# Load order, piece shapes and zero matmuls at the start of a cross-attention and maxout kernel

## The chip, the cores and the metric

The kernel runs on one core of one Trainium2 chip. The metric is the device time of one execution in microseconds (us); before the change it is 150.77 us (median of 3 runs, 150.74 to 151.8). TensorE is called PE here, its weight loads PEld, VectorE DVE, ScalarE ACT, GpSimd POOL; SyncE (SP) issues nearly all DMAs.

## What is computed

The reference, cut to what matters (B=8, H=8, S=512, Ns=32, D=64; the second part has d_model 512 and d_ff 1024):

```python
def _attn_ref(x, state):                       # x: B,H,S,D   state: B,H,Ns,D
    scores = scale * np.matmul(x, state.transpose(0, 1, 3, 2))
    ...                                        # softmax over the 32 state rows: a
    xread = np.matmul(a, state)
    scores2 = scale * np.matmul(state, x.transpose(0, 1, 3, 2))
    ...                                        # softmax over the 512 rows of x: a2
    sread = np.matmul(a2, x)
    return np.concatenate([xread, sread], axis=2)

def _moe_ref(x, w1, w2, w_out):                # x: 8 * 544 rows of 512
    h1 = x @ w1
    h2 = x @ w2
    g = np.maximum(h1, h2)
    return (g @ w_out)
```

The kernel uses max(h1, h2) = max(h1 - h2, 0) + h2. So it needs the difference of the two weights, `wd` = W1 - W2, and the product `wwo` = W2 Wo, and the output is relu(x wd) Wo + x wwo.

## The kernel before, in words

All loads are float32 and all matmuls take bfloat16. x is loaded per batch in two halves of four heads (`load_x(b, g)`, 512 KB each, runs of 1 KB in a partition). The weights come in pieces: `PIECES` (L19) gives for each of four pieces of W1 and of W2 the columns of d_ff and the blocks of 128 rows of d_model, 512 KB each, and Wo comes in quarters `load_wo(q)` of two blocks of 128 rows of d_ff. State is loaded for batch 0, for batch 1 and for batches 2 to 7.

The steps, by the short names that the order table uses:

- `ce` casts two heads of x to bfloat16 (`cast_e`, L209); `xt` transposes four heads on PE (8 matmuls), `xte` copies them out of PSUM. `cS`, `S`, `Se` do the same for the state.
- `sc` scores (8 matmuls), `exp` their exponential on ACT, `red` the sums and reciprocals on DVE, `mul` the normalised weights a; `at`/`ate` transpose a and copy it out. `sr`, `sre`, `srt`, `srte` are the read of x by the state. These give attention's parts of one batch.
- `cw2` casts a piece of W2, `w2` transposes it on PE (8 matmuls), `w2e` copies it to `w2m`. `cwo` casts a quarter of Wo. `ww.i.q` is two matmuls of the product `wwo`, for the block i of d_model and quarter q of d_ff; `wwe` copies a finished block.
- `sub.k.h` is half of piece k of the difference `wd` (`w_sub`, L414).
- `sw.b.z` multiplies the state of batch b by a range z of columns of `wd` (or, z = w, by `wwo`), 8 matmuls; `swe` copies it to `sw_s`. `CHUNKS` (L21) says which ranges batches 0 and 1 have.
- `l1.b.f` is two matmuls (L332) for block f of d_ff, `re` their relu. `l2.b.c.q` is two matmuls (L346) over quarter q, and `l2.b.c.o` two (L341) with `wwo`; five of them make an output block, which `le` copies out and `store` stores.

The work of batches 0 and 1 and of the preparation is not in a loop. The table `ORDER` (L23 to L46) is the order in which the instructions are issued; each engine gets its part of it in this order and waits in order. `@` gives the PSUM bank, `>` the engine (V, A, P for DVE, ACT, POOL). The loop for batches 2 to 7 follows (L573 on), and in it one l1 of 8 blocks, one l2 of 4 and the attention of the next batch. `idle` (L423) multiplies zeros, and `idle.9@0` at the start of the order is 9 such matmuls of 512 columns. `RELEASE` is the order in which the loop takes the eight banks.

The order of DMAs is that of SP's queue. Slots of `big` are used in turn: the fifth batch's x goes into the slot in which the first half of W2's columns was.

Of the kernel before, what the change touches and what calls it, by code (L numbers as in the profile page):

```python
# [23 lines left out]
cw2.2>P ldw2.1 sc.0.1@0 red.0.0>V exp.0.1>A w2.2@1 mul.0.0>P cw2.3>A sr.0@0 red.0.1>V ldw2.0 mul.0.1>P sre.0>V w2.3@2
cwo.3>A ldwo.0 w2e.2>V srt.0@0 at.0.0@3 srte.0>A sub.3.0>V w2e.3>A ldwo.1 sub.3.1>V ldw1.0 ate.0.0>A ww.2.3@2
sub.2.0>V ldw1.1 at.0.1@1 cS.1.2>A ww.3.3@3 ww.1.3@0 sub.2.1>V ate.0.1>A ldS.2.8 S.1.2@4 sw.0.1@1,5 Se.1.2.1>V
ce.1.3>A Se.1.2.0>V ce.1.2>P sw.1.1@4,6 swe.0.1.1>V ww.0.3@7 swe.0.1.0>A swe.1.1.0>V xt.1.1@5 swe.1.1.1>A ce.1.1>P
l1.0.7@1 ce.1.0>A xte.1.1>V l1.0.4@6 l1.0.6@4 re.0.7>A re.0.4>V cwo.2>P xt.1.0@5 re.0.6>A sc.1.1@1 l1.0.5@6 xte.1.0>V  # L30
exp.1.1>A ww.3.2@3 re.0.5>A sc.1.0@1 red.1.1>V ww.1.2@0 exp.1.0>A ww.2.2@2 cw2.1>V ww.0.2@7 l2.0.1.2@1 mul.1.1>P
ldx.3.1 red.1.0>V w2.1@6 cw2.0>A l2.0.2.2@5 mul.1.0>P w2e.1>V l2.0.2.3@5 l2.0.1.3@1 cwo.0>V w2.0@6 at.1.1@4 ww.2.0@2
w2e.0>V ldx.2.1 ww.3.0@3 cwo.1>P ate.1.1>V ww.0.0@7 ww.1.0@0 sub.0.1>V ldx.2.0 ww.3.1@3 at.1.0@4 ldx.3.0 sub.0.0>V
ww.0.1@7 wwe.3>A ww.1.1@0 sub.1.1>P ate.1.0>V wwe.0>A ww.2.1@2 wwe.1>V l1.1.7@7 wwe.2>A sr.1@4 sub.1.0>V re.1.7>A
sw.0.w@2,0 sre.1>V sw.0.0@3,6 swe.0.w.1>A l1.1.5@7 swe.0.w.0>V l1.1.6@4 swe.0.0.1>A mS.1>P l1.1.4@0 re.1.5>A re.1.6>V
l2.0.0.2@6 re.1.4>A l2.0.1.o@1 swe.0.0.0>V ce.3.2>P sw.1.0@4,7 mS.0>A sw.1.w@3,0 ce.3.3>P swe.1.0.1>V l2.0.0.3@6
swe.1.w.1>A cb.3.1>P Sd l1.0.0@2 swe.1.0.0>V l1.0.1@7 swe.1.w.0>A re.0.0>V l2.0.3.2@4 cb.2.1>P re.0.1>A l2.0.2.o@5
l1.1.1@2 ce.3.0>P l2.0.1.0@1 re.1.1>V l1.0.2@7 cb.2.0>P l1.1.3@3 re.0.2>V l2.0.3.o@4 re.1.3>A ce.3.1>P xtd.2 l1.1.0@2
ce.2.1>P l2.0.3.0@4 re.1.0>A srt.1@3 l2.0.0.0@6 ldx.4.0 cb.3.0>P srte.1>V l1.0.3@2 l2.0.0.o@6 re.0.3>A ce.2.2>P
l2.0.3.3@4 xtd.3 l1.1.2@2 ce.2.0>P l2.0.1.1@1 re.1.2>A ce.2.3>P l2.1.3.2@3 le.0.1>V l2.1.3.3@3 l2.1.3.1@3 l2.1.3.0@3  # L40
l2.1.2.2@1 ldx.4.1 l2.1.0.o@2 sc.2.1@7 l2.0.3.1@4 exp.2.1>A sc.2.0@0 l2.0.0.1@6 exp.2.0>A red.2.1>V l2.1.0.0@2
le.0.3>A l2.1.0.3@2 red.2.0>V mul.2.1>P l2.1.0.2@2 l2.1.2.3@1 le.0.0>V l2.1.2.o@1 mul.2.0>P l2.1.0.1@2 l2.0.2.0@5
le.1.0>A atd.2 l2.1.2.1@1 l2.0.2.1@5 l2.1.3.o@3 le.0.2>A l2.1.2.0@1 le.1.3>V sw.2.1@5,2 store.0 le.1.2>A sw.2.0@6,4
swe.2.1.0>V sw.2.w@3,0 swe.2.1.1>A sr.2@1 swe.2.0.0>V l2.1.1.3@5 swe.2.w.1>A l2.1.1.o@5 sre.2>V swe.2.0.1>A l2.1.1.2@5
l2.1.1.1@5 swe.2.w.0>V srt.2@1 l2.1.1.0@5 srte.2>V le.1.1>A
# [628 lines left out]
```

## Time and profile before

| what | us |
|---|---|
| median of 3 runs | 150.77 |
| the profiled execution's own time | 150.94 |
| its span, first to last instruction | 149.0 |
| around the span | 1.94 |
| PE busy in the span | 138.1 |
| from the start to the first l1 of batch 2 | 54.82 |
| from there to the end | 94.2 |

The tables of windows in the prediction give for a stretch of the span: its length, then for PE, PEld, DVE, ACT and POOL the busy time and the count of instructions, the clock granted to TensorE (1.00 is full), the busy share of the DMA engines, and GB/s. Rows of the timeline give the start, the duration, the engine, the line, the operation and, in brackets, how long the engine had been idle and what ended that; "x2" merges instructions that follow each other. In a row that starts after a wait for a DMA, the start is the landing of that DMA, within some 0.05 us. The chain's rows give start, duration and the step that the end was waiting for.

### The profile page before, as it was taken

To read this page: it belongs to the slowest core of one execution; us is meant where nothing else is said; L and a number is where in the kernel's file an instruction comes from. 1 tells how busy PE (TensorE), PEld (TensorE's weight loads), DVE (VectorE), ACT (ScalarE), POOL (GpSimd) and SP (SyncE) were. 2 spreads that over 40 slices of the span, in tenths; PEclk is the share of its full clock that TensorE was granted. 3 is DMA by queue.
4 is the path that set the end of the run, shared out by engine and by line. 5 is a ranking of instruction groups with operands and counts; after the bars stand their busy time and mean duration, and the time that the engine had idled before them with its cause. 6 is when DMAs were issued, how large, how long until landed. Compare 5 with 4: busy or idle time off the path is not lost.

```text
span 149.0 us, 3067 instructions
## 1 busy us (share of the span) xinstructions
PE 138.1 (93%) x1205; PEld 68.9 (46%) x1224; DVE 83.3 (56%) x163; ACT 66.1 (44%) x120; POOL 53.0 (36%) x81
## 2 busy tenths in 40 slices
PE   6846979999999999999999999999999999999990
PEld 2435446434445445444544454454445344754460
DVE  3567876796415367583855485376637586640120
ACT  3258673387324557045632745181547135511100
POOL 4352147497913700735091437056500500000000
PEclk9987999999999999999999999999999999999999
DMA  4999999996996568986969598779306033302332
GB/s 137 255 396 362 370 387 378 283 342 93 189 246 200 106 248 297 129 208 230 235 145 290 234 114 189 264 282 145 70 31 255 7 66 141 145 0 96 115 140 80
DMA packets 36063, 29.44 MB, mean 198 GB/s; under 512 B 23120, under 2 KB 31568, under 8 KB 35152
## 3 DMA queue, kind: packets, MB, share of 16 engines
q1 hardware_dynamic: 35776, 29.17, 69.9%
q8 instruction: 10, 0.16, 0.4%
q10 hardware_dynamic: 272, 0.07, 0.2%
q14 instruction: 5, 0.04, 0.1%
HBM read 15.20 MB, written 8.91 MB: 162 GB/s over the span
## 4 chain that ended last, share of the span: by engine, by line
PE 81%; DMA 10%; SPq 3%; DVE 1%; issue 1%; POOL 1%; ACT 0%
PE bank L346 38%; PE bank L332 17%; PE bank L341 9%; DMA big<-in_moe_w_out_dram 7%; PE bank L309 4%; PE bank L460 3%; DMA big<-in_x_dram 3%; SPq L155 3%; PE bank L365 2%; PE bank L375 2%; PE bank L240 2%; PE bank L280 1%; PE bank L373 1%; DVE wd L417 1%; POOL wo L103 1%
## 5 line engine op out<-in xcount | busy, mean ns | idle before, releaser
L346 PE MATMUL bank<-wo,r 128*128 128x512 bf16 (+1 forms) x259 | 61.4, 372 | 0.5
L346 PEld LDWEIGHTS <-r 128*128 128x128 bf16 x264 | 25.4, 98 | 28.5 <-issue 0.3
L99 ACT COPY big<-bank 128x512 f32<-128x512 f32 (+1 forms) x17 | 9.7, 573 | 47.1 <-PE bank L346 47.1
L332 PE MATMUL bank<-at,sw 128*128 128x512 bf16 x126 | 30.0, 379 | 0.1
L256 POOL TENSOR_TENSOR a<-e,er 128x512 bf16<-128x512 bf16 x16 | 16.7, 1065 | 36.3 <-ACT e L248 16.0
L327 DVE TENSOR_SCALAR r<-bank 128x512 bf16<-128x512 f32 x29 | 20.0, 691 | 15.9 <-PE bank L332 15.5
L325 ACT ACTIVATE r<-bank 128x512 bf16<-128x512 f32 x35 | 21.2, 608 | 8.2 <-PE bank L332 8.0
L101 DVE CAST sw<-bank 128x512 bf16<-128x512 f32 x24 | 15.3, 685 | 9.4 <-PE bank L309 9.3
L103 POOL CAST xe<-big 128x512 bf16<-128x512 f32 x28 | 16.4, 620 | 10.0 <-DMA big<-in_x_dram 10.0
L332 PEld LDWEIGHTS <-sw 128*128 128x128 bf16 x128 | 12.0, 98 | 14.0 <-issue 0.2
L101 DVE COPY big<-bank 128x512 f32<-128x512 f32 (+1 forms) x16 | 10.5, 654 | 13.6 <-PE bank L346 11.2
L341 PE MATMUL bank<-sw,at 128*128 128x512 bf16 (+1 forms) x56 | 17.1, 372 | 0.3
L103 POOL CAST xb<-big 128x1024 bf16<-128x1024 f32 x12 | 12.3, 1041 | 12.1 <-issue 11.4
L252 DVE TENSOR_REDUCE sums<-e 128x16 f32<-128x512 bf16 x16 | 10.6, 664 | 4.5 <-ACT e L248 4.4
L99 ACT CAST sw<-bank 128x512 bf16<-128x512 f32 x24 | 12.7, 599 | 0.2
L248 ACT ACTIVATE e<-bank 128x512 bf16<-128x512 f32 x16 | 9.0, 595 | 4.9 <-PE bank L240 4.5
L460 PE MATMUL bank<-wo,w2m 128*128 128x512 bf16 x30 | 7.8, 379 | 1.9 <-ACT w2m L99 1.2
L341 PEld LDWEIGHTS <-at 128*128 128x128 bf16 x66 | 5.7, 97 | 5.3
L240 PEld LDWEIGHTS <-xt 128*128 128x128 bf16 x128 | 5.1, 98 | 2.6 <-DVE xt L101 0.7
L240 PE MATMUL bank<-sbd,xt 128*128 128x64 bf16 x128 | 5.5, 193 | 0.6 <-DVE xt L101 0.6
L309 PE MATMUL bank<-wd,sbd 64*32 64x512 bf16 x128 | 5.8, 382 | 0.3 <-DVE sbd L101 0.2
L101 DVE COPY w2m<-bank 128x1024 bf16<-128x1024 bf16 (+1 forms) x4 | 2.8, 689 | 5.1 <-PE bank L375 4.1
(71 smaller groups left out, 105.1 us busy)
## 6 DMA issues: line engine op xcount, KB each, us to landing
big<-in_x_dram SPq DMA_DIRECT2D x14, 512.0 KB, 5.1
out_dram<-big SPq DMA_DIRECT2D x7, 1024.0 KB, 6.0
big<-in_moe_w_dram SPq DMA_DIRECT2D x8, 512.0 KB, 10.2
big<-in_moe_w_out_dram SPq DMA_DIRECT2D x4, 512.0 KB, 10.3
big<-in_x_dram SPq DMA_DIRECT2D x1, 1024.0 KB, 5.4
out_dram<-big SPq DMA_DIRECT2D x1, 512.0 KB, 2.6
out_dram<-w2m SPq DMA_DIRECT2D x2, 256.0 KB, 2.4
sf<-in_state_dram SPq DMA_DIRECT2D x1, 384.0 KB, 11.0
```

The lines of the kernel that those rows point to most:

```text
L99: nc.scalar.copy(o, i)
L101: nc.vector.tensor_copy(o, i)
L103: nc.gpsimd.tensor_copy(o, i)
L240: nc.tensor.matmul(pv[:, c, kk], xt_s[b % 2][:, c, k, :], sbd[:, b, k, :], start=(c == 0 and kk == 0), stop=(c == NC - 1 and kk == 1))
L256: (nc.gpsimd if eng == "P" else nc.vector).tensor_mul(e_view(a_s[b % 2], hh), e_view(e_s[b % 2], hh), er_s[b % 2][:, hh].unsqueeze(3).to_b ...
L309: nc.tensor.matmul(pg[g][32 * i:32 * i + 32, 0:n], sbd[64 * g:64 * g + 64, b, i, 32 * g:32 * g + 32], rhs, start=True, stop=True)
L325: nc.scalar.activation(out=o, in_=p, func=ACTF.Relu)
L327: nc.vector.tensor_scalar(o, p, scalar1=0.0, scalar2=None, op0=ALU.max)
L332: nc.tensor.matmul(p, sw_s[b % 3][:, g, f * 128:(f + 1) * 128], at_s[b % 3][:, g].rearrange("p c t -> p (c t)"), start=(g == 0), stop=(g = ...
L341: nc.tensor.matmul(p[:, lo:hi], at_s[b % 3][:, g, c, :], sw_s[b % 3][:, g, FF + lo:FF + hi], start=(start and g == 0), stop=(stop and g == 1))
L346: nc.tensor.matmul(p[:, lo:hi], r_s[b % 2][:, f, c * 128:(c + 1) * 128], wo[:, f, lo:hi], start=(start and j == 0), stop=(stop and j == le ...
L460: nc.tensor.matmul(p, w2t[:, f, i, :], wo[:, f, :], start=(first and f % 2 == 0), stop=(last and f % 2 == 1))
```

## The change

Four tables, one function and one entry of the table of steps are edited; the line numbers of the kernel move by 3.

1. `PIECES`: the two pieces of the first 512 columns of W1 and W2 are now 256 columns of all four row blocks (runs of 1 KB in DRAM) where they were 512 columns of two row blocks (runs of 2 KB). The two pieces of the other columns stay.
2. `CHUNKS`: batch 0 takes these two ranges of 256 columns one by one, so it has four `sw` where it had three.
3. `ORDER` is new: other order of loads, other engines for some steps, other banks. x1 and the state of batch 1 are loaded before any weight. Then come the two pieces of W2 of the first columns, the two quarters of Wo that belong to them, and one piece of W1.
4. `fill`: 30 matmuls of zeros, 16 of 512 and 14 of 256 columns, stand in PE's order: 12 ahead of the first transposes, 18 between the later ones up to the product `ww`. `idle.9@0` is gone.
5. `RELEASE` is another permutation.

```diff
-PIECES = [(0, 512, 0, 2), (0, 512, 2, 4), (512, 1024, 0, 2), (512, 1024, 2, 4)]
-
-CHUNKS = [[(0, 512), (512, 1024)], [(0, 512), (512, 1024)]]
+PIECES = [(0, 256, 0, 4), (256, 512, 0, 4), (512, 1024, 0, 2), (512, 1024, 2, 4)]
+
+CHUNKS = [[(0, 256), (256, 512), (512, 1024)], [(0, 512), (512, 1024)]]
...
-ldx.0.0 ldS.0.1 idle.9@0 ldx.0.1 ldw2.2 ldw2.3 ldwo.3 ldw1.3 ldw1.2 ldS.1.2 ce.0.0>V ce.0.1>P ldx.1.1 cS.0.1>V ldx.1.0
...
+ldx.0.1 ldS.0.1 fill.7@0 ldx.0.0 fill.111@1 ldS.1.2 fill.13@0 fill.9@1 fill.113@0 ldx.1.1 fill.102@1 ldx.1.0 fill.8@0
...
-RELEASE = [7, 2, 6, 0, 4, 3, 1, 5]
+RELEASE = [3, 2, 6, 5, 0, 7, 4, 1]
...
-    def idle(n, ring):
+    def idle(n, ring, w=512):
         p = bank(ring)
         for j in range(n):
-            nc.tensor.matmul(p, wz[:, 0:128], wz, start=True, stop=True)
+            nc.tensor.matmul(p[:, 0:w], wz[:, 0:128], wz[:, 0:w], start=True, stop=True)
...
-        idle=idle, cS=s_cast, mS=lambda z, e: s_mask(z, LATE, B, e), Sd=lambda: s_dma(LATE, B), ce=cast_e, cb=cast_b, xtd=xt_dma,
+        idle=idle, fill=lambda k, r: idle(1, r, 512 if k >= 100 else 256), cS=s_cast, mS=lambda z, e: s_mask(z, LATE, B, e), Sd=lambda: s_dma(LATE, B), ce=cast_e, cb=cast_b, xtd=xt_dma,
```

SP's queue from its first DMA, before. The names are those of the written and the read tensor; `in_moe_w` is W1 or W2, `big_113` holds the second columns of W2, `big_115` the second half of Wo, `big_114` the second columns of W1.

```order
L155 DMA big_109<-in_x_dram 128x4x256 x2
L163 DMA big_113<-in_moe_w_dram 128x2x512 x2
L167 DMA big_115<-in_moe_w_out_dram 128x2x512
L163 DMA big_114<-in_moe_w_dram 128x2x512 x2
L171 DMA sf_81<-in_state_dram 128x2x64
L155 DMA big_116<-in_x_dram 128x4x256 x2
L167 DMA big_115<-in_moe_w_out_dram 128x2x512
L163 DMA big_110<-in_moe_w_dram 128x2x512 x2
L167 DMA big_112<-in_moe_w_out_dram 128x2x512 x2
L163 DMA big_111<-in_moe_w_dram 128x2x512 x2
L171 DMA sf_81<-in_state_dram 128x12x64
```

The same place after the change; `big_110` and `big_111` hold the first columns of W2 and W1, `big_112` the first half of Wo, `big_116` is x1, `big_117` x2, `big_118` x3.

```order
L158 DMA big_109<-in_x_dram 128x4x256 x2
L174 DMA sf_81<-in_state_dram 128x2x64
L158 DMA big_116<-in_x_dram 128x4x256 x2
L166 DMA big_110<-in_moe_w_dram 128x4x256 x2
L170 DMA big_112<-in_moe_w_out_dram 128x2x512 x2
L166 DMA big_111<-in_moe_w_dram 128x4x256
L166 DMA big_113<-in_moe_w_dram 128x2x512 x2
L170 DMA big_115<-in_moe_w_out_dram 128x2x512 x2
L166 DMA big_111<-in_moe_w_dram 128x4x256
L166 DMA big_114<-in_moe_w_dram 128x2x512 x2
L158 DMA big_117<-in_x_dram 128x4x256 x2
L158 DMA big_110<-in_x_dram 128x4x256
```

What moved: x1 went from behind five weight pieces to ahead of all; the weights of the first columns went ahead of those of the second; half of x4 (the last row, into W2's slot) went ahead of the state of batches 2 to 7 and of x3.

ACT before, from its first exponentials (`e_91`) to the copies of a (`at_99`); `wb` is the cast piece of W2, `w2m` its transposed copy, `wo` the cast Wo:

```order
L248 ACTIVATE e_91<-bank_64 128x8x64
L248 ACTIVATE e_91<-bank_63 128x8x64
L99 CAST wb_108<-big_113 128x1024
L99 CAST wo_77<-big_115 128x1024
L99 COPY sread_t_78<-bank_63 128x4x32
L99 COPY w2m_80<-bank_65 128x4x256
L99 COPY at_99<-bank_66 128x512
```

ACT after, from the same exponentials:

```order
L251 ACTIVATE e_91<-bank_64 128x8x64
L251 ACTIVATE e_91<-bank_67 128x8x64
L102 CAST xe_85<-big_116 128x2x4x64
L102 COPY xt_88<-bank_63 128x4x256
L102 CAST wb_107<-big_110 128x1024
L251 ACTIVATE e_92<-bank_63 128x8x64
L251 ACTIVATE e_92<-bank_64 128x8x64
L102 COPY w2m_80<-bank_67 128x1024
L102 COPY w2m_80<-bank_65 128x1024
L102 CAST wo_77<-big_112 128x1024
```

What moved: batch 1's cast, its copy of the transposed x (`xt_88`) and its two exponentials (`e_92`) now stand among the steps of W2; both copies to `w2m` are ACT's, and come behind them.

More of the change, by code (lines that the diff above doesn't have):

```diff
@@ L26 @@
[L26 to L45, printed above, removed]
+ldx.0.1 ldS.0.1 fill.7@0 ldx.0.0 fill.111@1 ldS.1.2 fill.13@0 fill.9@1 fill.113@0 ldx.1.1 fill.102@1 ldx.1.0 fill.8@0
@@ new lines @@
+fill.14@1 ldw2.1 fill.108@0 ldw2.0 fill.107@1 fill.100@0 ce.0.2>V ce.0.3>A fill.105@1 cS.0.1>V xt.0.1@0 ldwo.1
+fill.103@1 ldwo.0 ce.0.1>A ce.0.0>V fill.104@2 ldw1.1 xte.0.1>V S.0.1@1 cS.1.2>A xt.0.0@2 Se.0.1.1>V Se.0.1.0>A
+S.1.2@0 fill.5@3 sc.0.1@1 xte.0.0>V Se.1.2.1>A fill.109@3 ldw2.3 fill.4@4 ce.1.2>P ce.1.3>A Se.1.2.0>V sc.0.0@4
+fill.112@0 ldw2.2 exp.0.1>A fill.114@2 xt.1.1@0 exp.0.0>A red.0.1>V ldwo.2 fill.15@1 fill.101@2 ce.1.1>P fill.110@1
+ce.1.0>A fill.12@2 sr.0@4 ldwo.3 red.0.0>V mul.0.1>P xte.1.1>A fill.115@2 ldw1.0 xt.1.0@1 sre.0>V fill.0@2 mul.0.0>P
@@ new lines @@
+fill.106@3 cw2.1>A fill.10@2 sc.1.1@0 xte.1.0>V cw2.0>P exp.1.1>A sc.1.0@1 ldw1.3 w2.1@4 exp.1.0>A red.1.1>V fill.2@0
+w2.0@2 w2e.1>A sr.1@1 cwo.1>V ldw1.2 fill.3@0 at.0.0@3 red.1.0>V mul.1.1>P w2e.0>A ww.2.1@0 ldx.2.1 ww.3.1@4 srt.0@5
+mul.1.0>V ww.1.1@6 cwo.0>A ww.0.1@2 sub.1.1>V fill.6@7 srte.0>A ww.2.0@0 ldx.2.0 sub.1.0>V ate.0.0>A ww.1.0@6 ww.3.0@4
+cw2.3>A sre.1>V at.0.1@3 ww.0.0@2 sw.0.1@1,5 ate.0.1>A w2.3@7 swe.0.1.1>V cw2.2>P swe.0.1.0>A at.1.1@3 w2e.3>V
+l1.0.3@1 ate.1.1>A w2.2@5 cwo.2>V re.0.3>A at.1.0@3 l1.0.2@7 w2e.2>V ww.2.2@0 re.0.2>A ww.3.2@4 cwo.3>V ww.0.2@2
@@ new lines @@
+ate.1.0>V ww.0.3@2 ww.1.3@6 sub.0.1>V wwe.0>A ww.1.2@6 ww.2.3@0 sub.0.0>V wwe.1>A l2.0.3.1@2 sub.3.1>P wwe.2>A ldx.4.1
+sw.0.0@6,3 sw.1.0@7,5 swe.0.0.1>V ldS.2.8 ww.3.3@4 swe.0.0.0>A swe.1.0.1>A l1.0.0@6 sub.3.0>V l1.0.1@3 swe.1.0.0>A
+sub.2.0>P wwe.3>V l2.0.2.1@5 re.0.1>A l1.1.1@7 ldx.3.0 l1.1.0@4 re.0.0>A sub.2.1>V l1.1.3@3 re.1.1>A re.1.0>V
+l2.0.2.0@5 cb.2.1>P re.1.3>A sw.0.2@7,6 sw.1.1@4,0 swe.0.2.1>A swe.0.2.0>V l1.1.2@3 ce.2.2>P l2.0.3.0@2 swe.1.1.1>A
+swe.1.1.0>V cb.2.0>P sw.0.w@7,6 re.1.2>A sw.1.w@0,1 swe.0.w.1>V l2.0.0.0@4 swe.1.w.1>A ce.2.1>P xtd.2 l1.1.7@3
@@ new lines @@
+swe.0.w.0>A ce.2.0>P l1.0.5@1 re.1.7>V l1.1.5@6 swe.1.w.0>A ldx.3.1 ce.2.3>P l2.0.3.o@2 re.0.5>V mS.1>A mS.0>P
+l1.0.7@0 re.1.5>V l1.0.6@1 re.0.7>A l1.0.4@3 re.0.6>V l2.0.2.o@5 re.0.4>A l1.1.6@0 Sd ce.3.1>P l2.0.0.1@4 re.1.6>V
+ldx.4.0 l1.1.4@3 ce.3.0>P l2.0.0.o@4 re.1.4>A cb.3.0>P l2.0.2.2@5 l2.0.3.2@2 l2.1.3.1@3 l2.1.3.o@3 l2.1.2.2@0
+l2.1.1.0@1 ce.3.2>P l2.1.1.3@1 ce.3.3>P l2.0.2.3@5 l2.1.2.1@0 cb.3.1>P le.0.2>A l2.1.0.0@6 l2.1.3.0@3 xtd.3 sc.2.1@5
+l2.1.3.2@3 exp.2.1>A l2.1.3.3@3 l2.0.3.3@2 red.2.1>V le.1.3>A l2.1.1.2@1 le.0.3>A l2.0.0.2@4 mul.2.1>P sc.2.0@3
@@ L46 @@
+l2.1.2.0@0 exp.2.0>A l2.1.0.o@6 l2.1.2.o@0 red.2.0>V l2.0.0.3@4 l2.1.0.1@6 le.0.0>A mul.2.0>P l2.1.1.1@1 l2.1.0.2@6
+atd.2 l2.1.0.3@6 l2.1.2.3@0 le.1.0>A sr.2@4 le.1.2>V sw.2.1@6,3 sw.2.w@2,5 sre.2>V swe.2.1.1>A sw.2.0@0,7 l2.1.1.o@1
+swe.2.1.0>V swe.2.w.0>A l2.0.1.o@4 swe.2.w.1>A l2.0.1.0@4 swe.2.0.0>V l2.0.1.1@4 swe.2.0.1>A le.1.1>V l2.0.1.3@4
+l2.0.1.2@4 srt.1@1 srt.2@7 le.0.1>A srte.2>V srte.1>A store.0
 """
```

1 line of the change is left out of this document (removed).

## The prediction

> **What bounds the kernel now.** I read the page first: what PE does in the 40 slices.
>
> ```profile
> PE 138.1 (93%) x1205; PEld 68.9 (46%) x1224; DVE 83.3 (56%) x163; ACT 66.1 (44%) x120; POOL 53.0 (36%) x81
> ...
> PE   6846979999999999999999999999999999999990
> ...
> PEclk9987999999999999999999999999999999999999
> ```
>
> PE is the bound from slice 6 on; only the first 20 us have gaps, and a lowered clock. Next the chain that ended last, up to the first l1 of batch 2 (its last row here):
>
> ```profile
> 9.95 10.21 DMA big<-in_moe_w_out_dram
> 20.21 1.05 POOL wo L103
> ...
> 25.60 0.45 PE bank L405 x8
> ...
> 29.55 0.69 DVE wwo L101
> 30.24 1.11 DVE wd L417
> ...
> 31.39 0.40 PE bank L309 x4
> ...
> 34.05 0.56 PE bank L309 x16
> ...
> 42.13 2.59 PE bank L346 x12
> ...
> 54.82 1.29 PE bank L332 x6
> ```
>
> Until 20.2 us the end waits for loads, then nearly only for PE. So what counts is when PE has real work without a break, and how much is left then. The 94.2 us behind 54.82 keep their instructions; I leave them as they are. The rows of PE give the unit prices: 2.59/12 = 0.216 us for a matmul of 512 columns, so 0.43 for one l1, l2 or ww, and 0.56/2 = 0.28 for one sw, 0.45 for one w2. Third, windows: four of the length of the clock's steps, two with loads in runs of 1 KB, one in runs of 2 KB, one at the first W2 piece, and the stretch that ends at 54.82.
>
> ```profile
> 3.03:6.44 3.41, 3.10 (x15) 1.37 (x14) 1.26 (x3) 0.16 (x1) 1.02 (x2) 1.00 1.01 293
> 6.44:9.86 3.42, 1.71 (x28) 1.13 (x26) 2.62 (x5) 1.91 (x4) 1.12 (x2) 1.00 0.96 338
> 9.86:13.27 3.41, 3.04 (x53) 2.46 (x53) 1.95 (x7) 2.40 (x4) 2.33 (x3) 0.50 1.06 389
> 13.27:16.68 3.41, 2.01 (x23) 1.05 (x24) 3.03 (x7) 2.84 (x6) 0.36 (x1) 1.00 1.10 348
> 5.50:7.50 2.00, 1.74 (x18) 1.40 (x19) 0.95 (x3) 0.88 (x2) 0.61 (x1) 1.00 0.79 182
> 14.60:15.60 1.00, 1.00 (x8) 0.56 (x8) 0.93 (x2) 0.95 (x3) 0.00 (x0) 1.00 1.10 349
> 20.00:25.00 5.00, 4.30 (x42) 2.47 (x40) 3.78 (x8) 3.15 (x5) 3.39 (x3) 1.00 1.05 387
> 31.39:54.82 23.43, 23.19 (x185) 10.73 (x189) 12.60 (x26) 11.87 (x21) 13.20 (x17) 1.00 0.79 203
> ...
> 27.50:30.00 2.50, 2.50 (x16) 1.20 (x14) 1.68 (x4) 1.19 (x3) 1.37 (x2) 1.00 1.07 301
> ```
>
> The load stream runs without a break. A 512 KB piece takes 524/349 = 1.50 us in runs of 1 KB (x here) and 524/387 = 1.35 us in runs of 2 KB. At 5.5 to 7.5, where the first W2 piece starts, the stream is at 182: 2.0 x (1 - 182/387) = 1.06 us are lost.
>
> Fourth, the timeline's rows for the other prices (a row with x2 is two instructions):
>
> ```profile
> 6.21 0.61 POOL L103 CAST xe<-big 128x512 bf16<-128x512 f32 x1 [0.82 <-DMA big<-in_x_dram]
> 7.95 0.60 ACT L248 ACTIVATE e<-bank 128x512 bf16<-128x512 f32 x1 [0.76 <-PE bank L240]
> 8.58 0.69 DVE L252 TENSOR_REDUCE sums<-e 128x16 f32<-128x512 bf16 x1
> 9.30 0.25 DVE L253 RECIPROCAL er<-sums 128x16 f32<-128x16 f32 x1
> 10.13 2.06 POOL L256 TENSOR_TENSOR a<-e,er 128x512 bf16<-128x512 bf16 x2
> 10.43 1.05 ACT L99 CAST wb<-big 128x1024 bf16<-128x1024 f32 x1 [0.90 <-DMA big<-in_moe_w_dram]
> 13.15 1.11 ACT L99 COPY w2m<-bank 128x1024 bf16<-128x1024 bf16 x1
> 13.21 1.29 DVE L417 TENSOR_TENSOR wd<-big,big 128x512 bf16<-128x512 f32 x2
> 14.54 0.38 PE L460 MATMUL bank<-wo,w2m 128*128 128x512 bf16 x1 [1.19 <-ACT w2m L99]
> 16.82 1.07 ACT L99 CAST sw<-bank 128x512 bf16<-128x512 f32 x2
> 24.95 0.68 DVE L101 CAST wo<-big 128x1024 bf16<-128x1024 f32 x1
> ```
>
> **The loads (the term that sets all else).** x0 and the first state have landed at 6.21 before. Now the state of batch 1 (64 KB, 66/349 = 0.19 us) and x1 (two pieces, 3.0 us) follow: 9.4. The first piece of W2, now in runs of 1 KB, adds 1.50, and the slow start of the W2 stream 1.06 if it comes again: 11.95. I call this landing M and take M = 11.95. Without the slow start it is 10.9; if strided 1 KB runs go as slowly as the slowest row of that kind (301, so 1.74 a piece), 12.2. Behind M stand, by the same prices: w2.0 at M+1.5, wo.1 M+2.85, wo.0 M+4.2, w1.1 M+5.7, w2.3 M+7.05, w2.2 M+8.4, wo.2 M+9.75, wo.3 M+11.1, w1.0 M+12.6, w1.3 M+13.95, w1.2 M+15.3.
>
> **From M to dense work on PE.** ACT in its new order: cast of W2 to M+1.1, the two exponentials of batch 1 to M+2.3, copy to `w2m` (1.11) to M+3.45. DVE has cast wo.1 at M+2.85 + 0.68 = M+3.55, so the first ww starts at M+3.6 = 15.55. PE's own steps before it (the transposes of W2, 0.45 each, sr and at of batches 1 and 0) fit into that time.
>
> From there PE has, up to the step sw.0.2 (the range of the second columns): 16 ww, 7 l1, 3 l2 at 0.43 = 11.2; two w2, three at (half as long as w2), three sw = 2.4; in all 13.7 with the last fill. It waits twice: for the cast of w2.3 (M+7.05 + 1.05 = M+8.1, PE is there at M+7.8: 0.3) and for ACT's copy of the first `sw` that stands behind that cast and a copy of a (0.35). With 0.2 for the semaphores of the stretch, sw.0.2 starts at M+18.1 = 30.05. What could hold it is the last W1 piece: M+15.3, then POOL and DVE take its halves, M+16.8. That has 1.3 us to spare. The other arrivals are closer: the casts of wo.2 and wo.3 and the halves of w1.0 on DVE end 0.15 to 0.3 us ahead of their use, so a stream that is later by more than that from M on goes straight into the sum.
>
> **What is left then.** Before, sw.0.0 starts at 31.39 with 11 l1, 36 l2 and 6 sw to do, and takes 23.43 (0.24 of it idle). Now sw.0.2 starts with 9 l1, 37 l2 and 7 sw; the scores, sr and srt that are left are the same. So 23.43 - 0.86 + 0.43 + 0.28 = 23.28. Two bank waits are new in it: `sw.1.w` and l1.0.5 wait for ACT's copies of the ranges before them, 0.3 by ACT's 0.53 a copy. The first l1 of batch 2 then starts at 30.05 + 23.3 + 0.3 = 53.6, against 54.82: 1.2 us earlier.
>
> **The zero matmuls.** The 12 at the start are 7 of 512 and 5 of 256 columns, as much as 9.5 of 512, against 9 before; the first x half with its casts is there as late as their end. The other 18 add up to 2.9 us (9 of 512, 9 of 256 columns at full speed) and all stand ahead of the first ww, where PE has under 5 us of real work to do in over 9 us: they cost nothing as long as loads and ACT set M+3.6. If that cover went, one of them delays a step by 0.1 to 0.2. What they may bring is the clock. Before, a window with 1.71 us of busy PE was followed by one at 0.50, one with 2.01 by one at 1.00; the slow window 9.86 to 13.27 costs about 1.1 us of PE time there (two w2 and one at at half speed), but PE idles at its end for loads anyway, so that is worth little. The point of decision lies between 1.71 and 2.01 of 3.41 us. After the change, I count 2.4 and 2.9 in windows with the same edges.
>
> The Trainium skill, "TensorE: Matmul & The Clock Gate", in "Why this matters for your kernels", has the clock fall only after an idle gap of some 3 us between bursts. By that rule the zeros bring nothing here and the clock rival below has no chance at all. This trace speaks against it: the longest gap ahead of the slow window is the next row's.
>
> ```profile
> PE bank L405 <- POOL wb L103: 1.3, 1, 1.3
> ```
>
> **Moved and added, at no cost.** *mul.1.0* goes to DVE, where no row shows it: between 0.65 (half the row of `wd`) and 1.03 (POOL's). DVE is then done by M+5.6, before w1.1 has landed: nothing either way. *The fourth sw* is in the count. *x4's half* now stands on SP ahead of the state of batches 2 to 7 and x3, and waits for the last subtraction from W2's first columns (M+14). Behind it wait the state and x3, but until M+18.3 = 30.2 the stream is busy with x2. The state then lands near 33, POOL masks it by 35.5, and its transposed copy (4.1 us to landing, below) is there at 39.6; PE reaches batch 2's scores near 42. So 2.4 us of cover; past that, each us is one. *store.0* is issued at the end of the order, not at 51; nothing reads it.
>
> ```profile
> sbd<-sb SPq DMA_TRANSPOSE x1, 4.1
> ```
>
> **Sum.** -1.2 us, with nothing behind 54.82 changed. The profiled execution took 150.94 (span 149.0, and 1.94 around it), so 149.7; it was 0.17 above the median of 150.77. Against the median: 149.5 us.
>
> **Rivals.**
> - *The slow start of W2 doesn't come again.* For it: the first piece of W1 and of Wo showed none, the stream was at 389 in 9.86 to 13.27 where they lay. Against: it came where W2 was first read, as it is now. M is 1.06 earlier and all that hangs on it: 148.4.
> - *The clock drops while ww runs.* Slower than before: one window of 3.41 us at half speed in which PE has 3.4 us of real work costs 1.7, so 149.5 + 1.7 = 151.2. It decides where a window that ends between M+2 and M+4 has less than about 1.9 us of busy PE. The edges of the windows need not lie as in this run; with edges at 11.2 and 14.6 I count 2.0, since PE then has only batch 1's scores, one w2 and three or four zeros. For: this thin stretch. Against: edges elsewhere give 2.4 and more. The Trainium skill, same page, Part 4, says that transposes do not count as busy; by that rule this rival would be the likely outcome, since w2 and at are transposes. The trace speaks against it: the 53 matmuls from 9.86 to 13.27 are 16 transposes of W2, 5 others and the 32 small ones of sr, and the next window is at 1.00.
> - *The weight pieces in 1 KB runs are slow.* The stride in DRAM is new, no row has it. At 301 the four pieces take 0.24 more each, 1.0 in all, with 0.2 of slack: 149.5 + 0.8 = 150.3.
> - *The change doesn't do what it says*: x1 is early but batch 1's attention is not used before M+8, so the early load only delays W2. That is in the sum: the first ww moves from 14.5 to 15.55, and what wins is that PE doesn't run dry behind it.
>
> **Chances.** My sum 0.46, with its own range 148.9 to 150.2 (loads 0.3 earlier or later, waits of 0.3 that I don't see). No slow start 0.23; clock 0.17; slow 1 KB runs 0.11; something else 0.03. From 148.2 to 151.5 holds all but the ends of each. A measurement of this kernel tells about 1% from no change, 149.26 and 152.28. Faster than that: the second case whole (0.23) and the lower third of mine (0.14): 0.37. Slower: the clock and slow runs together, or two slow windows, and what I don't see: 0.09. The rest 0.54.
>
> **What would show it.** In the changed kernel's profile: the first cast of W2 on ACT starts at 12.0 (10.9 or 12.2 in the rivals); the first matmul of L463 at 15.5; the first l1 of batch 2 at 53.6; the clock 1.00 from 6 or 7 us on (a window at 0.50 that covers 15 to 20 is the second rival); GB/s near 349 while W2's first columns load. I would be wrong if PE shows gaps of over 0.5 us between 20 and 30, or if batch 2's scores wait for the state.

## The result, and the profile after

| | before | after |
|---|---|---|
| median of 20 runs (us) | 151.03 | 150.84 |
| ratio, 95% interval | 1 | 0.9992 [0.9972, 1.0012] |
| the profiled execution (us) | 150.94 | 150.38 |
| first l1 of batch 2, in the chain | 54.82 | 54.22 |
| from there to the end of the last matmul | 90.2 | 90.2 |

No difference can be measured; the forecast was 1.2 us faster. Two single runs, one of after at 168.6 and one of an experiment at 499.85, are left out of the ratios. The changed kernel was timed once more among the experiments: 150.95, ratio 0.9992 [0.9966, 1.0018].

The page after, the same rows as were shown of before:

```profile
PE 140.7 (95%) x1253; PEld 69.7 (47%) x1253; DVE 80.6 (54%) x158; ACT 70.5 (47%) x130; POOL 51.3 (35%) x78
...
PE   6897889999999999999999999999999999999980
...
PEclk9999999999999999999999999999999999999999
```

PE is busier by 2.6 us and the span is only 0.4 shorter: by the prices of the prediction the 30 zeros are some 5 us of PE's busy time, where the nine of before were 2. The lowered clock at the start is gone. The chain of after, from the load that it follows to the first l1 of batch 2:

```profile
10.26 10.92 DMA big<-in_moe_w_dram
...
21.33 1.05 POOL wb L106
...
23.70 3.02 PE bank L463 x14
...
31.16 0.56 PE bank L312 x16
...
54.22 3.45 PE bank L335 x16
```

The end now follows the load stream until 21.2 us (the last piece of W2), 1.0 us later than before, and only then PE. sw.0.2 starts at 31.16; the forecast was 30.05. (The chain begins a step where the one before it ends. The record of the first l1 of batch 2 itself starts 0.16 earlier, at 54.06; the experiments are compared by these records.) The load stream itself, in the timeline: each of these rows starts when its DMA lands.

```profile
14.30 1.49 DVE L104 CAST wo<-big 128x1024 bf16<-128x1024 f32 x1 [0.26 <-DMA big<-in_moe_w_out_dram]
...
17.01 1.04 ACT L102 CAST wo<-big 128x1024 bf16<-128x1024 f32 x1 [1.27 <-DMA big<-in_moe_w_out_dram]
...
18.50 1.29 DVE L420 TENSOR_TENSOR wd<-big,big 128x512 bf16<-128x512 f32 x2 [1.11 <-DMA big<-in_moe_w_dram]
...
19.91 1.04 ACT L102 CAST wb<-big 128x1024 bf16<-128x1024 f32 x1 [1.08 <-DMA big<-in_moe_w_dram]
...
25.42 1.29 DVE L420 TENSOR_TENSOR wd<-big,big 128x512 bf16<-128x512 f32 x2 [0.47 <-DMA big<-in_moe_w_dram]
```

The rows are wo.1, wo.0, w1.1, w2.3 and w1.0. From w1.1 to w2.3 it takes 1.4, a piece's price; from wo.1 to wo.0 it takes 2.7, two pieces' price. In that gap the profile's table of DMA queues (14.2 to 17.1; columns: packets, MB, share of 16 engines) has

```profile
q1 hardware_dynamic: 788, 1.04, 104.1%
q8 instruction: 1, 0.02, 2.4%
```

The loads ran on at full rate (366 GB/s in that window), but one packet of 16 KB in the queue `instruction` took 1.11 us of one of the 16 engines. A DMA has landed when all 16 shares have. The trace's record of landings has fifteen shares of wo.0 by 15.67 and the last at 16.99; of w1.1, by 17.16 and at 18.48. So 15 engines go ahead by 1.32, about one piece, and every later landing of the weights up to w1.3 waits for the sixteenth. Before had this too: packet at 15.64, landing gap at x1's half (16.27 to 18.80). The Trainium skill, "DMA: Bandwidth & Descriptors", "Queues, rings and completion order", has each engine drain a whole packet from one queue's ring before it switches. The trace fits that: this packet took 1.11 us, and the late share came 1.32 behind the others.

The windows of after:

```profile
3.03:6.44 3.41, 3.41 (x19) 1.68 (x17) 0.63 (x3) 0.63 (x2) 0.00 (x0) 1.00 1.09 335
...
9.86:13.27 3.41, 3.04 (x71) 2.17 (x69) 2.90 (x9) 3.29 (x6) 2.96 (x4) 1.00 1.08 362
13.27:16.68 3.41, 2.67 (x56) 1.70 (x54) 3.07 (x5) 2.40 (x3) 1.79 (x2) 1.00 1.07 370
...
31.16:54.22 23.06, 23.06 (x200) 10.45 (x200) 10.16 (x19) 12.11 (x23) 13.78 (x17) 1.00 0.78 153
15.84:31.16 15.32, 14.56 (x114) 6.86 (x121) 11.59 (x21) 10.29 (x19) 5.26 (x4) 1.00 1.08 364
```

The clock is full throughout. From the first ww (15.84) to sw.0.2 PE is idle for 15.32 - 14.56 = 0.76 us, and from there to batch 2 not at all. So PE hardly waits; it does its steps in an order in which waits are short, yet each comes later than forecast, since the stream is later.

### The profile page after: what moved, and what is told of

It is laid out like the page before. It is cut to its first block, busy times and chain, and to the rows that moved or that the text cites. A ratio compares the mean times of both kernels' runs of the same rounds, so it can differ in the third digit from the quotient of the medians.

```text
span 148.6 us, 3146 instructions
## 1 busy us (share of the span) xinstructions
PE 140.7 (95%) x1253; PEld 69.7 (47%) x1253; DVE 80.6 (54%) x158; ACT 70.5 (47%) x130; POOL 51.3 (35%) x78
## 4 chain that ended last, share of the span: by engine, by line
PE 82%; DMA 7%; SPq 6%; POOL 1%; issue 1%; ACT 0%; POOLq 0%
PE bank L349 37%; PE bank L335 18%; PE bank L344 10%; DMA big<-in_moe_w_dram 7%; PE bank L312 4%; SPq L166 3%; PE bank L463 2%; PE bank L368 2%; PE bank L378 2%; PE bank L243 2%; PE bank L283 1%; SPq L158 1%; SPq L170 1%; PE bank L376 1%; POOL wb L106 1%
## 5 line engine op out<-in xcount | busy, mean ns | idle before, releaser
L330 DVE TENSOR_SCALAR r<-bank 128x512 bf16<-128x512 f32 x30 | 20.6, 691 | 15.2 <-PE bank L335 14.7
L259 POOL TENSOR_TENSOR a<-e,er 128x512 bf16<-128x512 bf16 x15 | 15.5, 1048 | 27.5 <-DVE er L256 15.9
L328 ACT ACTIVATE r<-bank 128x512 bf16<-128x512 f32 x34 | 20.6, 613 | 6.5 <-PE bank L335 6.1
L104 DVE CAST sw<-bank 128x512 bf16<-128x512 f32 (+1 forms) x22 | 13.5, 661 | 10.9 <-PE bank L312 10.7
L344 PE MATMUL bank<-sw,at 128*128 128x512 bf16 (+1 forms) x66 | 19.0, 374 | 0.0
L106 POOL CAST xb<-big 128x1024 bf16<-128x1024 f32 x12 | 12.8, 1077 | 17.1 <-issue 16.3
L106 POOL CAST xe<-big 128x512 bf16<-128x512 f32 x26 | 15.0, 612 | 9.8 <-DMA big<-in_x_dram 9.8
L104 DVE COPY big<-bank 128x512 f32<-128x512 f32 (+1 forms) x15 | 9.8, 656 | 11.2 <-PE bank L349 11.2
L102 ACT CAST sw<-bank 128x512 bf16<-128x512 f32 (+1 forms) x28 | 14.3, 585 | 1.0 <-PE bank L312 0.8
L429 PE MATMUL bank<-wz 128*128 128x512 bf16 (+1 forms) x30 | 8.8, 413 | 1.3 <-DVE ones L432 1.3
L312 PE MATMUL bank<-wd,sbd 64*32 64x512 bf16 (+1 forms) x136 | 5.4, 370 | 0.2 <-DVE sr L291 0.2
```

The costliest lines, as they stand in the source:

```text
L102: nc.scalar.copy(o, i)
L104: nc.vector.tensor_copy(o, i)
L106: nc.gpsimd.tensor_copy(o, i)
L259: (nc.gpsimd if eng == "P" else nc.vector).tensor_mul(e_view(a_s[b % 2], hh), e_view(e_s[b % 2], hh), er_s[b % 2][:, hh].unsqueeze(3).to_b ...
L312: nc.tensor.matmul(pg[g][32 * i:32 * i + 32, 0:n], sbd[64 * g:64 * g + 64, b, i, 32 * g:32 * g + 32], rhs, start=True, stop=True)
L328: nc.scalar.activation(out=o, in_=p, func=ACTF.Relu)
```

## The experiments

Two theories stood at first for the missing time: that the stream of loads sets the end of the first part, so that what makes a landing late (an instruction packet) costs its whole time; and that the zeros are not free, by the time they take on PE or by something else. All edits are to the changed kernel if not said otherwise. "Without the 18" leaves out the 18 zeros behind the first transposes.

| kernel | median us | ratio to before, 95% | 16 KB packet among the last stores, at us |
|---|---|---|---|
| after, again | 150.95 | 0.9992 [0.9966, 1.0018] | 142.52 |
| without the 18 | 150.13 | 0.9947 [0.9926, 0.9969] | none |
| the same, again | 150.22 | 0.9946 [0.992, 0.9972] | none |
| before with 10 zeros | 150.95 | 0.9998 [0.9969, 1.0026] | none |
| 76 small zeros first | 150.21 | 0.9949 [0.9928, 0.9971] | none (131.19) |
| sr moved, 9 zeros | 151.83 | 1.0036 [1.0012, 1.006] | none |
| 9 zeros only | 150.44 | 0.9968 [0.993, 1.0006] | none |
| no load of x1 | 149.3 | 0.9871 [0.9837, 0.9905] | 140.69 |
| without the 18, sre.1 first | 150.27 | 0.9943 [0.9919, 0.9967] | none |
| the 18 made small | 150.81 | 0.9983 [0.9955, 1.0011] | 141.76 |
| without the 18, 20 small first | 150.9 | 0.999 [0.9962, 1.0019] | 142.29 |
| without the 18, 76 small first | 151.36 | 1.0027 [0.9996, 1.0057] | none (132.32) |
| nine zeros cut in four | 150.3 | 0.9965 [0.9938, 0.9992] | none (134.64) |
| without the 18, 9 more small | 150.29 | 0.9937 [0.9915, 0.9959] | none |
| with the 18, 31 more small | 150.19 | 0.9933 [0.9907, 0.9959] | none (134.40) |

The last column is the start of the packet in the trace's record of packets; in brackets, that the same packet came earlier, ahead of the last stores. (Every kernel has one more behind its last matmul, at 143.9 to 146.9.) The ratios compare with runs of the kernel before that were taken beside each experiment; their medians are 151.10 to 151.27.

### First: the zeros, the clock, the packet

**Without the 18.**

```diff
-fill.103@1 ldwo.0 ce.0.1>A ce.0.0>V fill.104@2 ldw1.1
+ldwo.0 ce.0.1>A ce.0.0>V ldw1.1
...
-w2e.0>A ww.2.1@0 ldx.2.1 ww.3.1@4 srt.0@5 mul.1.0>V ww.1.1@6 cwo.0>A ww.0.1@2 sub.1.1>V fill.6@7
+w2e.0>A ww.2.1@0 ldx.2.1 ww.3.1@4 srt.0@5 mul.1.0>V ww.1.1@6 cwo.0>A ww.0.1@2 sub.1.1>V
```

> The changed kernel without the 18 zero matmuls that stand between real steps; the 12 at the start stay. Theory A (the load stream decides: in the changed kernel's trace every landing from wo.0 on is 1.2 us late, from the moment at 14.44 us when a 16 KB instruction packet goes through one of the 16 DMA engines, as at 15.64 before): 36 fewer PE instructions let that packet come later, near 16 us, so that wo.0 lands near 15.7 instead of 16.99 and the jump falls on w1.1 or w2.3; the time is 0 to 0.4 us less than the changed kernel's 150.84, if the clock stays. Theory B (the zeros hold the clock, and that is what the change lives on): a window with under 1.9 us of busy PE is followed by one at 0.50, and the time is 0.5 to 1.7 us more than the changed kernel's.

Measured 150.13, 0.7 less than after; a second time 150.22. Neither theory had this: B asked for more time, and A for 0.4 less at most, with the packet near 16. It starts at 14.66 (14.44 in after), and the gap is still at wo.0. Most of the forecast's gain is there, and the 18 zeros take it away again. The clock stayed at 1.00. Yet in the profiles the first part ends at the same time: first l1 of batch 2 at 54.00 without, 54.06 with them. What the zeros cost does not lie in the first part of these two traces, nor does it show in these two executions as wholes: 150.44 without, 150.38 with them.

**Before with 10 zeros in its waits.**

```diff
-sc.0.0@1 xte.0.1>V exp.0.0>A
+sc.0.0@1 fill.100@7 xte.0.1>V exp.0.0>A
...
+fill.101@7 fill.102@6 fill.103@7 fill.104@6 fill.105@7
...
+fill.106@7 fill.107@6 fill.108@7 fill.109@6
```

> The kernel before with ten zero matmuls of 512 columns in its early waits (one behind sc.0.0, five behind sc.0.1, four ahead of the first product ww) and nothing else changed. Theory B: clock 1.00 from about 6 us on, time 0.5 to 1.1 us less than before. Theory A: the clock stays at 1.00 too, but PE waits for the same landings as before, so the time is within 0.3 us of before; the 20 more PE instructions bring the 16 KB packet forward by about 1 us, to 14.6.

Measured 150.95, ratio 0.9998. The clock stays at 1.00 from 5.1 on, where before had a window at 0.50, and nothing is gained: as the prediction said, PE waits for loads at the end of that window anyway.

**76 small zeros at the start, the 18 kept.**

```diff
-fill.7@0
...
-fill.105@1
+tiny.76@0
...
+    def tiny(n, ring):
+        p = bank(ring)
+        for j in range(n):
+            nc.tensor.matmul(p[0:32, 0:64], wz[:, 0:32], wz[:, 0:64], start=True, stop=True)
```

> The changed kernel with its first 12 zero matmuls replaced by 76 small ones (32 x 64), about as long in time and 128 PE instructions more; same loads in the same order. Theory A: the 16 KB packet comes when PE has issued as many instructions as it had at 14.44, which is now near 10 to 11 us, and the long gap between two landings moves with it from wo.0 (14.28 to 16.99) to w2.0 or wo.1; from wo.0 on the landings are as in the changed kernel; the first ww starts about 1.2 us later (17.0 instead of 15.84) and the time is 0.2 to 0.8 us more. Rival C (the gap belongs to the first access to a tensor or to the fourth-quarter switch to Wo): the gap stays between wo.1 and wo.0 and the time is that of the changed kernel.

More PE instructions bring the first packet from 14.44 to 9.95, and the gap in the landings moves with it, from wo.0 to the first W2 piece (x1 at 9.89, w2.1 at 12.91). So more PE instructions bring the packet earlier, though not at one fixed count: the trace has 253 matmuls and weight loads ahead of it here, 287 in after. w1.0 still landed at 25.53: moved ahead, the gap delays all the same.

Measured 150.21, 0.6 less than after, where theory A had 0.2 to 0.8 more and rival C no change. This stayed open until the third part. The profiled execution, 151.31, is not typical: it lost the clock from 15.46 to 18.88, and its first l1 of batch 2 comes at 55.19.

**sr of batches 0 and 1 later, nine zeros at the start and no others.** Unlike what the expectation says, its output is not the reference's.

```diff
-sr.0@4
...
-sre.0>V
...
-sr.1@1
...
-srt.0@5
...
-srte.0>A
...
-sre.1>V
...
+l2.0.0.0@4 sr.0@7 sre.0>V
...
+l1.0.4@3 srt.0@7 srte.0>A
...
+l2.0.0.1@4 sr.1@7 sre.1>V
```

> The changed kernel with idle.9 at the start and no other zero matmul, and with the reads sr.0 and sr.1 (64 matmuls and their weight loads) and their evictions moved behind the landing of all weights; same loads. It computes all of the reference. Theory A: over 150 fewer PE instructions stand ahead of the first ww, so the 16 KB packet comes near 20 to 22 us; wo.0, w1.1, w2.3 and w2.2 land 1.2 us earlier than in the changed kernel (15.7, 17.1, 18.5, 19.8), PE reaches sw.0.2 near 30.2 instead of 31.2, and the time is 0.5 to 1.0 us less than the changed kernel's. Rival C: landings as in the changed kernel, time within 0.3 us of it. Theory B: without zeros the clock falls in one or two windows and the time is 0.5 to 1.7 us more.

With fewer PE instructions ahead of the weights the first packet comes at 18.23, and the gap follows again (from 18.66 to 21.50, at w2.2). But the clock was lost from 12.38 to 15.79, so the time, 151.83, says nothing on the packet alone.

### Second: does the stream set the end?

**After, unchanged.** 

> The changed kernel, unchanged, beside the others of this call on one chip, to tell whether the 0.6 us that its profile shows at the first l1 of batch 2 (54.22 against 54.82) is in its timed runs, and whether the kernel without zeros between real steps (150.13 against 151.12) is truly faster than it. If the zeros between steps cost nothing: 150.1 to 150.3, with a ratio to before near 0.995. If they cost: 150.6 to 151.0.

Measured 150.95, ratio 0.9992. In this execution the first x landed 0.7 later (5.34), and everything in the first part is later by that much.

**Nine zeros only, as before has them.**

```diff
-fill.7@0
...
-fill.6@7
+idle.9@0
```

> The changed kernel with idle.9 at the start in place of its 12 zero matmuls, and no other: the layout and the order alone. Theory A (the load stream sets when PE has work; zeros matter little): within 0.3 us of the kernel that lacks only the 18 (150.13); the 16 KB packet near 15 us, one landing gap of 2.3 to 2.8 us among wo.0, w1.1 and w2.3, all the later landings as in the changed kernel within 0.3 us. Theory B (zeros hold the clock): a window at 0.50 between 9 and 20 us and 0.5 to 1.7 us more.

Measured 150.44, with runs from 149.65 to 151.68. The profiled one lost the clock for two windows, and its first l1 of batch 2 came at 55.26, 1.26 after that of the kernel without the 18. Its windows:

```profile
8.92:12.33 3.41, 1.93 (x57) 1.34 (x54) 2.01 (x7) 3.37 (x6) 2.22 (x3) 1.00 1.09 355
12.33:15.74 3.41, 2.93 (x36) 2.31 (x38) 2.51 (x6) 2.97 (x4) 3.01 (x4) 0.50 1.07 378
```

and the thinnest of the kernel without the 18, which kept it:

```profile
11.90:15.31 3.41, 2.07 (x64) 1.68 (x64) 2.69 (x8) 3.23 (x6) 3.15 (x4) 1.00 1.07 380
```

So with x1 early a lost clock does cost, and in the two profiles of the kernel without the 18 the zeros ahead of the first transposes suffice against it, if barely.

**No load of x1.** Batch 1 reads x0's slot, so its part of the output is not the reference's.

```diff
-ldx.1.1
...
-ldx.1.0
...
+    slot["x1"] = slot["x0"]
```

> The changed kernel without the two loads of x1; batch 1 is computed from x0's slot, so the output of batch 1 is left wrong. The stream of weights starts 3.0 us earlier (w2.1 near 8.4 instead of 11.43, w1.2 near 25.1 instead of 28.14). Theory A (the stream sets the end of this part): first ww near 12.9 instead of 15.84, and the time is 1.5 to 2.9 us less than the changed kernel's. Rival (PE's own work or the engines that cast set it): 0 to 0.6 us less.

Measured 149.3, 1.65 less than after beside it. W1's third piece (w1.0) and the first l1 of batch 2:

```profile
23.01 1.29 DVE L422 TENSOR_TENSOR wd<-big,big 128x512 bf16<-128x512 f32 x2 [0.24 <-DMA big<-in_moe_w_dram]
```

```profile
52.18 3.45 PE bank L337 x16
```

The stream is 2.4 earlier at w1.0 than in after (25.42), and the end of the first part 2.0 earlier. In ten profiles at full clock the first l1 of batch 2 starts 28.63 to 28.90 behind the landing of w1.0, however PE's waits ahead of it fall (29.04 here). The load stream sets the end of the first part: shown. But w1.0 is only a mark on the stream. No table of PE's waits has a wait for it; in all ten the last wait ahead of 32 us is for ACT's cast of w2.3, four pieces earlier, and the chain of after leaves the stream at w2.2. Here PE waits for no piece between 15 and 32, so its own work holds the other 0.4.

**Without the 18, and sre.1 ahead of sub.1.1 on DVE.**

```diff
-ww.0.1@2 sub.1.1>V srte.0>A
+ww.0.1@2 sre.1>V sub.1.1>V srte.0>A
```

> The changed kernel without its 18 zeros between steps, and with DVE's eviction of sr.1 moved ahead of the two subtractions of w1.1 (it stood behind them, and sw.0.1 waits for its bank: a wait of 0.4 us of PE at 20.1). Theory A: the next step, the transposes of w2.3, waits for its landing and cast either way, so no gain: within 0.2 us of the kernel without the 18. Rival (the wait is on the path): 0.3 to 0.4 us less.

Measured 150.27, as without that edit (150.13, 150.22). It moves PE's waits (0.80 at 17.38 and 0.56 at 20.52, where the kernel without the 18 has 0.47 at 15.81 and 0.27 at 20.53), and the first l1 of batch 2 stays (54.12): the wait at 17.38 costs nothing, since PE then waits for the cast of w2.3 either way (its transposes start at 21.08, in after at 21.01).

### Third: what of the 18 zeros costs 0.65 us?

**The 18 made small** (64 columns on 32 rows: as many instructions, little PE time).

```diff
-fill.103@1 ldwo.0 ce.0.1>A ce.0.0>V fill.104@2 ldw1.1
+tiny.1@1 ldwo.0 ce.0.1>A ce.0.0>V tiny.1@2 ldw1.1
```

> The changed kernel with its 18 zero matmuls between steps shrunk to 32 x 64 (some 0.03 to 0.05 us each in place of 0.11 to 0.22), in the same places and the same number of PE instructions. What is open: the timed runs say that the 18 cost 0.6 to 0.8 us (150.95 with them, 150.13 and 150.27 without), and the two profiles with and without don't show where. Theory D (their time on PE costs): near 150.2. Theory E (their number costs, since 36 more PE instructions bring the second 16 KB packet from 26.1 to 24.9-25.4 us, ahead of the landing of w1.0, on which the end hangs): near 150.9.

Measured 150.81. The same cost with almost none of the columns: theory D, that their time on PE costs it, falls.

**Without the 18, but 20 small ones in the place of two zeros at the start** (as many PE instructions as after, none in the later waits).

```diff
-fill.100@0
...
-fill.105@1
+tiny.20@0
```

> The kernel without the 18, but with 20 zero matmuls of 32 x 64 in place of two of the 512-wide ones at the start (1.07 against 0.85 us): as many PE instructions as in the changed kernel, none of them between the steps. Theory E: second 16 KB packet near 25 us and 150.7 to 151.0. Theory D: 150.1 to 150.3, wherever the packet falls.

Measured 150.9. The place does not matter either; the number does. And in this trace the first l1 of batch 2 comes at 53.63, 0.4 earlier than in after, and still the execution took 151.01. The loss is behind it. The loop takes the same 13.85 a batch, and from the record of the first l1 of batch 2 to the end of the last matmul all 17 profiles of this case take the same 90.38. So it can only lie behind the last matmul: from there to the end of the span this kernel takes 5.09, the one without the 18 takes 4.25. The table of queues for 139.0 to 144.2 and the stores issued there (the last number is from issue to landing), first of this kernel:

```profile
q8 instruction: 1, 0.02, 1.1%
...
out_dram<-w2m SPq DMA_DIRECT2D x1, 256.0 KB, 4.4
```

the same of the kernel without the 18, which has no `q8` row in this window:

```profile
q1 hardware_dynamic: 354, 0.66, 33.6%
q14 instruction: 1, 0.01, 0.8%
...
out_dram<-w2m SPq DMA_DIRECT2D x1, 256.0 KB, 2.4
```

and the same of after:

```profile
q8 instruction: 1, 0.02, 1.5%
...
out_dram<-w2m SPq DMA_DIRECT2D x1, 256.0 KB, 3.6
```

Then the last store of all (144.3 on), of the kernel with 20 small ones first:

```profile
out_dram<-big SPq DMA_DIRECT2D x1, 128.0 KB, 3.7
```

and of the one without the 18:

```profile
out_dram<-big SPq DMA_DIRECT2D x1, 128.0 KB, 2.9
```

36 PE instructions more (18 matmuls, each with its weights) make the tenth packet of 16 KB start 1.7 to 2.8 us before the last matmul ends, in the middle of the last stores. Without the 18 no packet starts between 122 us and the end of the last matmul; the tenth comes behind it, at 145.2.

**Without the 18, 76 small ones first.**

```diff
-fill.7@0
...
-fill.105@1
+tiny.76@0
```

> The kernel without the 18, and with the first 12 replaced by 76 of 32 x 64 (as in the run that brought the first packet to 9.95 us and took 150.21 with the 18 in place). Theory D: 0.4 to 0.8 us less than that run, 149.4 to 149.8. Theory E: about the same, 150.0 to 150.3, since both packets (10 and 20 us) fall ahead of w1.0 but only the first shows in its landing.

Measured 151.36; the profiled one lost the clock from 16.01 to 19.43. It does not answer the question, but shows the price of the clock: first l1 of batch 2 at 55.04, 1.0 later than without the 18 (54.00).

**Without the 18, again.** 

> The kernel without the 18 once more, as a control on the same chip and for a second profile of it: 150.1 to 150.3 if the first was typical; its landing of w1.0 plus 28.6 to 28.8 us is the start of the first l1 of batch 2, as in every profile so far with a full clock (25.40 and 54.06, 26.09 and 54.75 for the changed kernel; 25.19 and 54.00 for this one).

Measured 150.22: the first result holds. In its profile the first l1 of batch 2 (53.94) is again 28.65 behind w1.0 (25.29).

That left two places that move with the number of PE instructions: the second packet (24.9 in after, 26.1 without the 18), ahead of w1.0 (theory E in the expectations), and the one among the last stores (theory T). The last three kernels part them.

**The nine later zeros of 512 columns cut in four each.**

```diff
-fill.103@1
...
-fill.115@2
+cut.103@1
...
+cut.115@2
...
+        for j in range(n * parts):
+            v = w // 4 if parts == 4 else w
+            nc.tensor.matmul(p[:, 0:v], wz[:, 0:128], wz[:, 0:v], start=True, stop=True)
```

> The changed kernel with the nine zero matmuls of 512 columns among the 18 later ones cut into four of 128 columns each: the same columns, 27 matmuls more. Theory T (the cost of the 18 zeros lies at the end: an extra instruction packet of 16 KB falls at 141.6 to 142.5, among the last stores): 54 more PE instructions bring this packet to about 136, ahead of the last stores, which then land 2.5 to 2.9 after their issue; time 150.2, ratio to the kernel before 0.995. Theory E (the second packet, ahead of W1's third piece, costs it): more instructions bring that packet still further ahead, time 150.8 or more, ratio 0.999 or more.

Measured 150.3: 27 matmuls *more* than after, and 0.5 to 0.65 below its two medians. (By the ratios it is 0.27%, and the two intervals still overlap.) The second packet came at 19.93, still further ahead of w1.0; the tenth came at 134.64.

**Without the 18, nine more at the start.**

```diff
-fill.105@1
+tiny.10@1
```

> The changed kernel without the 18 later zeros, and with one of 256... 512 columns at the start replaced by ten of 64 columns on 32 rows: nine matmuls more than the kernel without the 18, half of what the 18 add. Theory T: the extra packet fires at about 143.5, right in front of the last store, which lands 3.3 or more after its issue; time 150.7 to 151.0, ratio 0.998, as with all 18. Theory E: the second packet moves half as far ahead (to about 25.5), time 150.5, ratio 0.997.

Measured 150.29. The count was set too low: the tenth packet did not come at all, so this is not the test that theory T asked for. But the second packet came at 25.51, as theory E wanted it, and the time is that of 26.1: against E.

**With the 18, 31 more at the start.**

```diff
-fill.107@1
...
-fill.100@0
...
-fill.105@1
+tiny.34@0
```

> The changed kernel with all 18 later zeros, and with three zeros of 512 columns at the start replaced by 34 of 64 columns on 32 rows: 31 matmuls more. Theory T: the extra packet fires at about 135.5, ahead of the last stores; time 150.2, ratio 0.995. Theory E: the first and second packets move to about 12.5 and 22.5, time 150.8 or more, ratio 0.999 or more.

Measured 150.19. Its tenth packet, in the table of queues from 131 to 139, stands beside stores that take no longer for it:

```profile
q8 instruction: 1, 0.02, 0.8%
...
out_dram<-big SPq DMA_DIRECT2D x1, 512.0 KB, 2.6
out_dram<-w2m SPq DMA_DIRECT2D x1, 256.0 KB, 2.5
```

and its last store lands in

```profile
out_dram<-big SPq DMA_DIRECT2D x1, 128.0 KB, 2.5
```

Theory E falls, and theory T has two of its forecasts borne out (150.2 both times) and one not tested. Four medians of kernels whose tenth packet falls at 141.6 to 142.5 lie at 150.81 to 150.95; seven of the new order without it there lie at 150.13 to 150.30: 0.65 between their means (150.88 and 150.23). Left out are the kernels without x1's load, with sr moved, with nine zeros only and with 76 small ones and no others; the last three lost the clock in their profiles. (So did the one with 76 small zeros and the 18, which is among the seven; eight of its ten runs, though, lie at 150.04 to 150.52.)

What stays open is the place of the loss in after itself. From the end of the last matmul to the end of the span the twelve profiles without a packet among the last stores take 3.86 to 4.29. Of the five with it three take longer: 4.71 with the 18 made small, 5.09 with 20 small ones first, 5.36 without x1's load; their last store lands 3.3, 3.7 and 3.8 behind its issue. But after and its repetition take 4.14 and 3.98 (last store 2.7 and 2.6), with only the store of 140.7 late. So the two profiles of the changed kernel show no loss there. That its timed runs lose their 0.65 by the last stores is inferred from the kernels in which the packet was moved.

The seven versions without a packet among the last stores have lower medians than both kernels: 150.13 to 150.30, ratios to before 0.9933 to 0.9965, each with its interval below 1.

## Why the prediction was wrong, step by step

**The step that failed is "they cost nothing", on the 18 zeros.** The working looked at PE's time in the waits, and there it holds: made small they cost as much. It did not count them as instructions that have to be fetched. In timed runs they cost 0.65, two thirds of what the rest of the change brings (the seven medians lie 0.9 to 1.1 below that of before beside them). That their number does it, and not their time or place, is shown by the kernels that shrink, move, add and cut zeros. In all of them the time goes with where the tenth packet falls; that after loses it at the last stores is inferred.

**"Behind M stand, by the same prices" failed by one packet.** The prices of a piece were right: 1.50 and 1.36, and the W2 pieces in runs of 1 KB ran as fast as x. But a stream of four x halves and twelve weight pieces met an instruction packet, and the sum of prices left it out, though before's landings had shown it. By the forecast's own prices w1.0 would have landed 12.6 behind M; it landed 13.97 behind: 1.37, the gap at wo.0. "A stream later than that goes straight into the sum" was right: 28.65 behind w1.0 comes batch 2.

**M was too late.** 11.95 forecast, 11.43 measured; the first cast of W2 on ACT started at 11.47. The slow start of W2 did not come again, as the first rival had it; x1 was 0.5 later than forecast. This gave back 0.5 of the packet's 1.37.

**The cast of wo.1** was priced at 0.68 and took 1.49, so the first ww started at 15.84, 4.4 behind M and not 3.6 (the last section shows why). It cost nothing: wo.1 itself landed 2.85 behind M, as forecast, and PE waits for the cast of w2.3 later either way. From the landing of w2.3 to sw.0.2 the forecast had 11.05; it took 11.33.

**The left work** was 23.58 forecast and 23.06 measured: the two bank waits of 0.3 did not come, and the price of the remaining steps was 0.2 too high. So 31.16 + 23.06 = 54.22 instead of 53.6, and the profiled gain was 0.6 of the 1.2. The sum over the first part is then, in rounded figures: M 0.5 earlier, the packet 1.4 and PE's work 0.3 later, the left work 0.5 shorter, together 0.6 later than forecast. This is one profile; the timed runs without the 18 gain more, 0.9 to 1.1, and why is not shown.

**Waits of PE** between 15.8 and 31.2, in the table of waits (us in total, times, longest):

```profile
PE bank L463 <- DVE wo L104: 0.4, 1, 0.4
PE bank L408 <- ACT wb L102: 0.3, 1, 0.3
PE bank L312 <- DVE sr L291: 0.2, 1, 0.2
PE bank L463 <- ACT wo L102: 0.2, 1, 0.2
```

The wait for the cast of w2.3 (0.3) is there as forecast. The one for the copy of `sw` is not; those for sr and for the late wo.0, 0.2 each, were not forecast. None is over 0.5, as the forecast asked.

**The rivals.** Slow 1 KB runs: out (351 GB/s from 10.00 to 11.40, where W2's first columns load). The clock: not in after, but without zeros in the waits it was close. Of windows at full clock, those with 1.39 (76 small first), 1.73 (76 small and the 18), 1.93 (nine zeros only) and 1.95 us (sr moved) of busy PE were followed by one at 0.50, and those with 1.97 and more were not (in before the bounds were 1.71 and 2.01). But the busy time alone does not decide it: with 20 small zeros first a window with 1.94 (9.81 to 13.23) was followed by one at 1.00, and with nine zeros only one with 2.93, itself at 0.50, by another at 0.50. The price of one lost window in the profiles is 1.0 to 1.1 (55.04 against 54.00, 55.19 against 54.06), and 1.26 for two, not 1.7. That "what they may bring is the clock" was worth little in before: right (0.9998). State and x4's move: no wait for them shows; batch 2's scores start at 43.55 and the state landed at 34.15.
